# Attention, token and channel mixing, Fourier mixing: the mixing pass's second layer sums three features per addition instead of two

## The chip, the cores and the metric

The kernel runs on one core of a Trainium2 chip. The core has TensorE (PE, with its weight loads PEld), VectorE (DVE), ScalarE (ACT), GpSimd (POOL) and SyncE (SP, whose queue issues the DMA transfers). What counts is the device time of one execution in microseconds (us). PE writes its products into PSUM, an on-chip memory of banks of 128 x 512 fp32 numbers; DVE and ACT carry them on to SBUF.

## The reference, cut to what matters

```python
q_pool = q.reshape(B, H, S // 2, 2, D).mean(axis=3)          # B 4, H 8, S 1152, D 64
scores = scale * np.matmul(q_pool, k.transpose(0, 1, 3, 2))
attn = softmax(scores)
x = np.matmul(attn, v)                                       # -> x: 4 x 576 x 512
# token and channel mixing
h = np.maximum(x.transpose(0, 2, 1) @ w_tok1, 0.0) @ w_tok2  # 576 -> 256 -> 576
u = x + h.transpose(0, 2, 1)
x = u + np.maximum(u @ w_ch1, 0.0) @ w_ch2                   # 512 -> 1536 -> 512
# Fourier mixing, normalisation, a second channel layer
u = x + np.real(fft(fft(x, axis=1), axis=2))
un = (u - mean(u)) / np.sqrt(var(u) + 1e-6)
out = u + np.maximum(un @ w2_ch1, 0.0) @ w2_ch2              # 512 -> 2048 -> 512
```

## The kernel before, in words

All numbers are fp32. A product of full precision is made of three products of a faster format (fp32r): each operand is split into a high part, which ACT writes, and a low rest, which DVE or POOL writes; PE adds high x high, high x low and low x high in PSUM. So "three matmuls" below is one product.

The work has these parts:

- **Conversion** (`conv64`): the weights arrive as 64-bit floats and are turned into pairs of fp32r by ACT, POOL and DVE during the attention, and stored to DRAM.
- **Attention**, 32 heads in turn, 8 to a batch. From the ninth head on (`peaks`, `unit`) PE makes a tile of scores (L644, six matmuls into a region `m` of three banks), DVE finds each row's maximum (L651), ACT takes the exponent (L654) into a tile `s`; only then is `m` free for the next tile. PE turns `s` (L797, into a shared bank or the bank `tr`), ACT writes the high part `ph` (L801) and DVE the low part `pl` (L804), and PE multiplies both with the values into the one bank `av` (L811). ACT and DVE carry `av` to `xtr` (L821, L823), PE turns that (L843), DVE scales it (L855), and ACT and POOL write the batch's input of the mixing pass as `x` high and low (L858, L860).
- **Mixing pass** (`mix`), one for each of the 4 batches; the pass of a batch runs while the next batch's attention does, the last one with the Fourier part. Its PE work is a chain in one fixed order: the token layer (`r`, L916, then `u`, L944 and L951, with the sum `yt` begun from `u`), and then the channel layer with its 1536 features in 12 blocks of 128. First layer of block f: 12 + 12 matmuls (L981; tokens 0 to 255 and 256 to 575 apart, as everywhere here), then ACT (L902) and DVE (L905) write the block's high and low part to a buffer `h`. Second layer: for each of the two token ranges and four output blocks, PE sums two features' three matmuls each in one bank (six matmuls, L1001), and one DVE addition (L1010) adds the bank to `yt`. So six bursts of eight such groups make a pass. At its end `yt` is turned (L1035) and written out by ACT (L1040).
- **Fourier mixing, normalisation and the last channel layer** (L1157 to L1503) follow.

`banks` is a ring of three PSUM banks, from which `r`, `u`, the two channel layers, half of the turned scores and the turned heads all take. The buffers `h` are a ring of three, `ph` and `pl` rings of five, and the mixing weights come through a ring of five buffers `w` (L458, 512 KB each for the channel layer), which SP loads in the chain's order.

What stands where in each engine's queue is decided by a planner (`Plan.order`): it walks through all operations with assumed costs, and gives a free engine the ready operation with the smallest due time. The table `SHIFT` adds a number for each kind of operation to its due time; the numbers are so large that they act as priorities. On PE the second mixing layer (`yT`) goes ahead of scores (`M`) and of turning (`T`); the products with the values (`AV`) come behind these, and the first mixing layer (`hT`) last.

Of the kernel before, what the change touches and what calls it, by code (L numbers as in the profile page):

```python
# [11 lines left out]
F32R = mybir.dt.float32r  # L12
# [9 lines left out]
B, H, S, D = 4, 8, 1152, 64  # L22
# [9 lines left out]
PB = 5  # L32
# [7 lines left out]
NB = 3  # L40
NC = 2
NW = 5
NV = 3
NS = 6
ALONE = 8
NPH = 5
NPL = 5
UNITS = ((0, 256, (0, 1), ((0, 1), (2, 3), (4, 5), (6, 7), (8,))),
         (256, 320, (2, 3, 4), tuple((c,) for c in range(9))))
SPANS = ((0, 256), (256, 320))  # L50
# [9 lines left out]


SHIFT = {
    "cvld": -25.93, "cabs": 1270.21, "cclamp": 705.49, "cshift": 902.44, "csign": -44.94, "cexp": 832.42,
    "cword": 774.03, "cmul": -558.47, "cadd": 708.59, "chi": -53.24, "csub": -115.78, "cvst": -413.51, "cs":
    73.61, "warm.": -140.63, "l.": -1704.02, "q.": 351.07, "qh.": 1553.78, "ql.": 797.09, "kh.": -19.45, "kl.":
    1892.97, "M.": -2130.55, "mr.": 433.1, "zh.": -685.21, "mr2.": -1605.04, "zl.": -866.61, "mT.": 452.86,
    "mrow.": -843.49, "vld": -524.16, "S.": -408.9, "exp.": 741.3, "AV.": -1055.77, "xe.": -17.83, "turn":
# [7 lines left out]
    -425.22, "open": -1557.19, "sqrt": -2175.63, "fcld": -988.57, "fchi": 736.12, "fclo": -782.79, "nyld":  # L75
    -1351.45, "nyh": 186.74, "fld": 108.37, "FPUT": 625.26, "DFT": 33.71, "Zh": 1221.35, "Zl": 1190.62, "PB":
    -31.25, "PA": -31.11, "bs": -454.93, "pm": 280.63, "yadd": -483.73, "u2st": 617.43, "dwld": -491.2, "dwv":
    109.22, "dwh": -1442.53, "dwl": 2012.18, "mixover": -388.78, "fnetover": 785.38, "uld": -771.51, "bn":
    183.78, "bnr": 707.04, "un": 1261.22, "dturn": -317.55, "dth": -715.08, "dtl": -2596.93, "L": 157.31, "drl":
    185.99, "dll": 484.72, "dadd": 481.33, "dst": -84.03, "TB": 538.99, "TH": 2063.54, "TL": -508.2, "TA":  # L80
    641.51, "WR": 855.14, "WH": 262.43, "WL": -497.16, "VR": -355.27, "LP": 206.65, "LE": 459.2, "LC": -1185.38,
    "LH": 628.53, "LL": 257.54, "LQ": 1903.14,
}
PACE = 1.0307

# [147 lines left out]
def tile_attention_moe_fnet(  # L233
# [51 lines left out]
    with tc.manual_schedule():  # L285
# [52 lines left out]

        flow = [(0, 0), (0, 1), (0, 2)]
        for f in range(0, F1, 2):
            flow += [(1, f), (1, f + 1)] + [(0, x) for x in (f + 3, f + 4) if x < F1]
        cvw = Ring(NV, lambda: shelf.tile([128, 2048], F32, tag="slot", name="slot", bufs=NV))
        converted = []

# [516 lines left out]
            return turn, [a, o]  # L863


        h_r = ring(3, mp, [128, 2, NQ], F32R, "h")
        ut_r = ring(1, mp, [128, 2, 4, NQ], F32R, "ut")
        yt_r = ring(1, mp, [128, 4, NQ], F32, "yt")
        yo_r = ring(3, mp, [128, C], F32, "yo")
# [2 lines left out]
        def mix(b, xx, x_ops):  # L872
# [119 lines left out]
                    ]))  # L992

            def layer2(f):
                ww = {x: get((1, x)) for x in (f, f + 1)}
                for r, (t0, n) in enumerate(SPANS):
                    for cc in range(4):
                        mms = []
                        for x in ww:
                            for wi, hi in ((0, 0), (0, 1), (1, 0)):  # L1000
                                mms.append(lambda ps, k=len(mms), x=x, wi=wi, hi=hi, cc=cc, t0=t0, n=n: nc.tensor.matmul(  # L1001
                                    ps[:, :n], ww[x][2]("p (s n) -> p s n", s=2)[:, wi, 128 * cc:128 * cc + 128],
                                    hs[x][0].t[:, hi, t0:t0 + n], start=(k == 0), stop=(k == 5)))

                        def y(cc=cc, t0=t0, n=n):
                            return yt.t[:, cc, t0:t0 + n]

                        deps = [ww[x][0] for x in ww] + [o for x in ww for o in hs[x][1][r]]
                        y_ops[r] += group("y", mms, t_pe(1, n), deps, [ww[x][1] for x in ww] + [hs[x][0] for x in ww], [
                            ("V", t_dve(n), lambda ps, y=y, n=n: nc.vector.tensor_tensor(  # L1010
                                out=y(), in0=ps[:, :n], in1=y(), op=ALU.add), [], u_ops[r], [yt])])

            for layer, f in flow:
                if layer == 0:
                    layer1(f)
                elif f % 2 == 0:
                    layer2(f)

            y_stores, rest = [], list(chain)
# [679 lines left out]
```

## Time and profile before

| | |
|---|---|
| median of three runs (lowest, highest) | 1431.44 us (1429.68, 1437.26) |
| the profiled execution | 1428.16 us |
| its span, first to last instruction | 1426.2 us |
| PE busy in the span | 1379.3 us, 97% |
| DVE, ACT, POOL busy | 988.5, 763.6, 576.6 us |

The span is what the profile's rows divide up; the profiled execution's own time is 2.0 us more. An engine is busy while an instruction of it runs; PE's matmuls overlap, so that its mean duration of one is longer than the time from one to the next.

### The profile page before, as it was taken

What the parts mean: (1) busy time and instruction counts of PE and PEld (TensorE: products, weight loads), DVE (VectorE), ACT (ScalarE), POOL (GpSimd) and SP (SyncE); (2) the same over time, 40 slices, a digit from 0 to 9 for tenths busy, and PEclk for the clock granted to TensorE, in tenths of its full rate; (3) what the DMA queues carried; (4) which work ended last, traced back from release to release, by engine and by line L of the source; (5) the groups of instructions that cost most, each with busy time, mean ns of one, the idle gap of its engine ahead of it and who ended that gap; (6) DMA issues with size and microseconds to landing.
All of it is one profiled execution on the core that took longest, in us unless ns stands there. A gap on an engine that the chain in (4) does not pass through costs nothing.

```text
span 1426.2 us, 24338 instructions
## 1 busy us (share of the span) xinstructions
PE 1379.3 (97%) x9019; PEld 1270.3 (89%) x9019; DVE 988.5 (69%) x1830; ACT 763.6 (54%) x1534; POOL 576.6 (40%) x471
## 2 busy tenths in 40 slices
PE   7999999999999999999999999999999999999998
PEld 6777788999988999999989998999899898888887
DVE  7667578978877789786878885577647665455443
ACT  4555568767667866656866654322325443344332
POOL 4667767756755557666354665021210000000000
PEclk8999999999999999999999999999999999999999
DMA  6676776776578577667754457875266543644532
GB/s 183 195 217 195 208 202 201 226 233 206 155 222 259 150 215 245 201 204 229 202 182 141 148 177 251 255 230 157 67 213 210 194 140 141 215 165 142 201 113 91
DMA packets 112176, 270.34 MB, mean 190 GB/s; under 512 B 9971, under 2 KB 37748, under 8 KB 111767
## 3 DMA queue, kind: packets, MB, share of 16 engines
q1 hardware_dynamic: 112058, 268.79, 60.9%
q8 instruction: 71, 1.16, 0.3%
q14 instruction: 47, 0.39, 0.1%
HBM read 191.15 MB, written 44.86 MB: 165 GB/s over the span
## 4 chain that ended last, share of the span: by engine, by line
PE 86%; DVE 6%; ACT 3%; issue 2%; DMA 1%; POOL 1%; SPq 0%; ACTq 0%; DVEq 0%; POOLq 0%
PE bank L981 10%; PE bank L1001 10%; PE bank L1444 10%; PE m L644 9%; PE av L811 7%; PE y L1503 7%; PE c L1503 5%; PE av L758 4%; PE bank L797 4%; PE tr L797 3%; PE bank L678 3%; PE s L747 2%; PE bank L1314 2%; PE y L1336 2%; PE bank L916 2%; PE c L1157 2%
## 5 line engine op out<-in xcount | busy, mean ns | idle before, releaser
L651 DVE TENSOR_REDUCE nm<-m 128x1 f32<-128x1152 f32 (+1 forms) x120 | 162.4, 1353 | 49.2 <-PE m L644 47.6
L981 PE MATMUL bank<-ut,w 128*128 128x320 f32 (+1 forms) x1152 | 177.2, 298 | 5.0 <-DVE h L905 2.0
L981 PEld LDWEIGHTS bank<-ut,w 128*128 128x128 f32 x1152 | 160.2, 190 | 7.1 <-DVE h L905 2.6
L1001 PE MATMUL bank<-h,w 128*128 128x320 f32 (+1 forms) x1152 | 164.4, 297 | 1.0 <-DVE yt L1010 0.7
L1444 PE MATMUL bank<-tt,wc 128*128 128x320 f32 x1008 | 157.7, 311 | 4.3 <-DVE e L1458 3.8
L644 PE MATMUL m<-kk,qq 128*128 128x384 f32 (+1 forms) x720 | 156.7, 349 | 4.6 <-ACT s L654 4.4
L1444 PEld LDWEIGHTS bank<-tt,wc 128*128 128x128 f32 x1008 | 150.0, 188 | 11.9 <-DVE e L1458 8.9
L1001 PEld LDWEIGHTS bank<-h,w 128*128 128x128 f32 x1152 | 157.3, 189 | 2.7 <-DVE yt L1010 1.3
L654 ACT ACTIVATE s<-m,nm 128x1152 f32<-128x1152 f32 (+1 forms) x120 | 146.2, 1218 | 18.4 <-DVE nm L651 17.9
L368 POOL TENSOR_SCALAR slot<-slot 128x512 f32<-128x512 f32 (+2 forms) x62 | 119.7, 1935 | 55.6 <-ACT slot L366 46.6
L811 PE MATMUL av<-ph,vv 128*128 128x256 f32 (+1 forms) x432 | 131.2, 321 | 4.5 <-DVE xtr L823 4.4
L644 PEld LDWEIGHTS m<-kk,qq 128*128 128x128 f32 (+1 forms) x720 | 119.1, 182 | 10.6 <-ACT s L654 6.5
L801 ACT ACTIVATE ph<-bank 128x512 fp32r<-128x512 f32 (+1 forms) x192 | 89.6, 470 | 71.5 <-PE bank L797 69.8
L381 POOL TENSOR_TENSOR slot<-slot 128x512 f32<-128x512 f32 (+2 forms) x62 | 80.7, 1302 | 102.4 <-DVE slot L376 98.6
L811 PE MATMUL av<-pl,vv 128*128 128x256 f32 (+1 forms) x432 | 120.4, 296 | 1.3 <-DVE pl L804 1.3
L1458 DVE TENSOR_TENSOR e<-bank,e 128x320 f32<-128x320 f32 x96 | 47.1, 491 | 106.4 <-PE bank L1444 70.7
L1010 DVE TENSOR_TENSOR yt<-bank,yt 128x256 f32<-128x256 f32 (+1 forms) x192 | 86.0, 454 | 41.0 <-PE bank L1001 38.6
L1503 PE MATMUL y<-v,hp 128*128 128x512 f32 x432 | 103.9, 390 | 0.0
L804 DVE TENSOR_TENSOR pl<-bank,ph 128x512 fp32r<-128x512 f32 (+1 forms) x192 | 99.0, 522 | 3.1 <-ACT ph L801 2.7
L1454 ACT ACTIVATE e<-bank 128x320 f32<-128x320 f32 x72 | 31.3, 434 | 129.4 <-PE bank L1444 129.4
L801 ACT ACTIVATE ph<-tr 128x512 fp32r<-128x512 f32 (+1 forms) x144 | 70.4, 489 | 54.5 <-PE tr L797 44.9
L804 DVE TENSOR_TENSOR pl<-tr,ph 128x512 fp32r<-128x512 f32 (+1 forms) x144 | 79.2, 550 | 26.3 <-ACT ph L801 25.7
(162 smaller groups left out, 2956.9 us busy)
## 6 DMA issues: line engine op xcount, KB each, us to landing
w<-wb_d SPq DMA_DIRECT2D x96, 512.0 KB, 5.5
slot<-in_wm_dram SPq DMA_DIRECT2D x56, 512.0 KB, 6.0
v<-w_d SPq DMA_DIRECT2D x24, 1024.0 KB, 5.6
raw<-w_d SPq DMA_DIRECT2D x24, 896.0 KB, 5.7
kk<-kx SPq DMA_DIRECT2D x66, 288.0 KB, 5.1
wb_d<-slot SPq DMA_DIRECT2D x24, 512.0 KB, 2.6
v<-in_v_dram SPq DMA_DIRECT2D x32, 292.5 KB, 5.7
kx<-in_kT_dram SPq DMA_DIRECT2D x15, 576.0 KB
```

What stands on the lines that cost most here:

```text
L368: a = add("cclamp", "P", 0.155 + n * 0.00347, due, lambda: nc.gpsimd.tensor_scalar(out=f32(hi()), in0=f32(hi()), scalar1=F64_LO, scalar2=F ...
L644: nc.tensor.matmul(m.t[:n, :KW], qq.t[:r, t, q0:q0 + n], kk.t[:r, c * KW:(c + 1) * KW], start=(t == 0), stop=(t == 1))
L651: a = add("mx" + own_place, "V", t_dve(S), d + 0.05, lambda n=n, j=j: nc.vector.tensor_reduce(out=nm.t[:n, j:j + 1], in_=m_tile[0][:n, :, ...
L654: o = add("exp" + own_place, "A", t_act(S) + 0.18, d + 0.1, lambda s=s, n=n, j=j: nc.scalar.activation(out=s.t[:n].rearrange("p (c n) -> p ...
L797: nc.tensor.transpose(ps.t[:, at:at + r], made[j][0].t[:r, c * 128:(c + 1) * 128], ident[:r, :r])
L801: a = add("hi", "A", t_act(n), due + 0.1, lambda ps=ps, ph=ph, n=n: nc.scalar.activation(out=ph.t[:, :n], in_=ps.t[:, :n], func=AF.Copy), ...
L804: b = add("lo", "V", t_dve(n), due + 0.2, lambda ps=ps, ph=ph, pl=pl, n=n: nc.vector.tensor_tensor(out=pl.t[:, :n], in0=ps.t[:, :n], in1=f ...
L811: nc.tensor.matmul(po.t[:, :nq], vv.t[:, c].rearrange("p s d -> p (s d)"), x.t[:, k * nq:(k + 1) * nq], start=c == 0 and x is ph, stop=c = ...
L981: mms.append(lambda ps, k=len(mms), kk=kk, wi=wi, xi=xi, t0=t0, n=n: nc.tensor.matmul(ps[:, :n], view("p (s k n) -> p s k n", s=2, k=4)[:, ...
L1001: mms.append(lambda ps, k=len(mms), x=x, wi=wi, hi=hi, cc=cc, t0=t0, n=n: nc.tensor.matmul(ps[:, :n], ww[x][2]("p (s n) -> p s n", s=2)[:, ...
L1444: nc.tensor.matmul(ps.t[:, :PH], w.t[:, wi, k, 128 * kk:128 * kk + 128], x.t[:, xi, kk], start=(first and m == 0), stop=(last and m == 5), ...
L1503: nc.tensor.matmul(y.t, h.t[:, k, hi, j * 128:(j + 1) * 128], v.t[:, wi, k], start=(q == 0 and k == 0 and n == 0), stop=(q == 7 and k == 1 ...
```

## The change

The second layer now sums three features in a bank (nine matmuls) for each addition to `yt`. The order of the mixing chain follows: four first layers, then bursts of 72 second-layer matmuls with three first layers between them, where there were bursts of 48 with two between them. The ring `h` gets a fourth buffer; the rings `ph` and `pl` have four instead of five. All numbers of `SHIFT` are new, those of a kind mostly near the old ones; `PACE` and the rings `banks` and `w` stay.

```diff
+YF = 3
-NPH = 5
-NPL = 5
+NPH = 4
+NPL = 4
...
 SHIFT = {
-    "cvld": -25.93, "cabs": 1270.21, "cclamp": 705.49, "cshift": 902.44, "csign": -44.94, "cexp": 832.42,
+    "cvld": -90.22, "cabs": 1239.90, "cclamp": 939.59, "cshift": 946.77, "csign": -127.29, "cexp": 940.57,
...
-        flow = [(0, 0), (0, 1), (0, 2)]
-        for f in range(0, F1, 2):
-            flow += [(1, f), (1, f + 1)] + [(0, x) for x in (f + 3, f + 4) if x < F1]
+        flow = [(0, f) for f in range(YF + 1)]
+        for f in range(0, F1, YF):
+            flow += [(1, f + x) for x in range(YF)] + [(0, f + x) for x in range(YF + 1, 2 * YF + 1) if f + x < F1]
...
-        h_r = ring(3, mp, [128, 2, NQ], F32R, "h")
+        h_r = ring(YF + 1, mp, [128, 2, NQ], F32R, "h")
...
-                ww = {x: get((1, x)) for x in (f, f + 1)}
+                ww = {x: get((1, x)) for x in range(f, f + YF)}
...
-                                    hs[x][0].t[:, hi, t0:t0 + n], start=(k == 0), stop=(k == 5)))
+                                    hs[x][0].t[:, hi, t0:t0 + n], start=(k == 0), stop=(k == 3 * YF - 1)))
...
-                elif f % 2 == 0:
+                elif f % YF == 0:
```

What this moves is seen in the engines' queues. The names are those of the section on the kernel; in the changed kernel every line number is one higher (L1002 for L1001).

PE, in the first mixing pass, where a second-layer burst meets the attention. Before:

```order
L843 MATMUL bank<-ident,xtr_130 128x65 x5
L1001 MATMUL bank<-h,w 128x256 x6
L644 MATMUL m<-kk_147,qq_154 66x384 x4
L1001 MATMUL bank<-h,w 128x256 x12
L1001 MATMUL bank<-h,w 128x320 x12
L644 MATMUL m<-kk_147,qq_154 66x384 x2
L797 MATMUL tr<-ident,s 128x128 x4
L1001 MATMUL bank<-h,w 128x320 x12
```

The same place with the change:

```order
L982 MATMUL bank<-ut,w 128x320 x12
L645 MATMUL m<-kk_147,qq_154 128x384 x6
L1002 MATMUL bank<-h,w 128x256 x36
L1002 MATMUL bank<-h,w 128x320 x36
L645 MATMUL m<-kk_147,qq_154 128x384 x6
L798 MATMUL tr<-ident,s 128x128 x2
L798 MATMUL tr<-ident,s 128x66
L798 MATMUL bank<-ident,s 128x128 x2
```

Score matmuls (L644), a turned head (L843) and turned scores (L797) stood inside the burst of 48; the burst of 72 stands in one piece, with a whole tile's six score matmuls ahead of it and six behind it.

PE at the end of the attention, the last head's last products with the values and what follows. Before:

```order
L811 MATMUL av<-ph,vv 128x320
L811 MATMUL av<-pl,vv 128x320
L981 MATMUL bank<-ut,w 128x320 x9
L1001 MATMUL bank<-h,w 128x256 x3
L843 MATMUL bank<-ident,xtr_132 128x65 x5
L1001 MATMUL bank<-h,w 128x256 x21
L1001 MATMUL bank<-h,w 128x320 x24
L981 MATMUL bank<-ut,w 128x256 x12
L981 MATMUL bank<-ut,w 128x320 x12
L1001 MATMUL bank<-h,w 128x256 x24
L1001 MATMUL bank<-h,w 128x320 x24
L1035 MATMUL bank<-ident,yt 96x128 x4
```

With the change:

```order
L812 MATMUL av<-pl,vv 128x320
L812 MATMUL av<-ph,vv 128x320
L812 MATMUL av<-pl,vv 128x320
L812 MATMUL av<-ph,vv 128x320
L812 MATMUL av<-pl,vv 128x320
L1036 MATMUL bank<-ident,yt 96x128 x4
L1036 MATMUL bank<-ident,yt 97x128 x4
L1036 MATMUL bank<-ident,yt 96x128 x4
L812 MATMUL av<-ph,vv 128x320
L812 MATMUL av<-pl,vv 128x320
L844 MATMUL bank<-ident,xtr_132 128x65 x5
L917 MATMUL bank<-x_8802,w 128x512
```

Before, 117 matmuls of the third mixing pass (L981, L1001) stood between the last turned head (L843) and the turning of `yt` ahead of the fourth pass. Now the third pass is finished by then: only the turning of `yt` (L1036) is left between the last products with the values, and the fourth pass's first layer (L917) stands directly behind the turned head (L844), whose result it reads.

PE at the beginning of the third mixing pass, where the token layer ends (L944, L951) and two heads of the next batch, which wait for the pass to give its input `x` back, are turned. Before:

```order
L797 MATMUL tr<-ident,s 128x66
L644 MATMUL m<-kk_145,qq_148 128x384 x2
L843 MATMUL bank<-ident,xtr_130 128x65 x5
L644 MATMUL m<-kk_145,qq_148 128x384 x4
L843 MATMUL bank<-ident,xtr_132 128x65 x5
L811 MATMUL av<-ph,vv 128x320
L811 MATMUL av<-pl,vv 128x320
L811 MATMUL av<-ph,vv 128x320
L811 MATMUL av<-pl,vv 128x320
L797 MATMUL bank<-ident,s 128x128 x2
```

With the change:

```order
L952 MATMUL bank<-ident_r,x_5647 128x64
L945 MATMUL bank<-w,h 128x320
L798 MATMUL tr<-ident,s 128x128 x2
L798 MATMUL tr<-ident,s 128x66
L844 MATMUL bank<-ident,xtr_130 128x65 x5
L844 MATMUL bank<-ident,xtr_132 128x65 x5
L645 MATMUL m<-kk_145,qq_148 128x384 x6
L798 MATMUL bank<-ident,s 128x128 x2
L798 MATMUL bank<-ident,s 128x66
```

The two turned heads (L843) stood inside a tile of scores, with products with the values (L811) right behind; they now stand together, and a tile of scores and turned scores come ahead of those products.

## Rows read from the trace of the kernel before

**Rows 1.** the first part of the page: busy time, share and instructions of each engine.
```profile
PE 1379.3 (97%) x9019; PEld 1270.3 (89%) x9019; DVE 988.5 (69%) x1830; ACT 763.6 (54%) x1534; POOL 576.6 (40%) x471
```

**Rows 2.** windows, whole stages: busy us (x instructions), clock, DMA share.
```profile
0.00:177.00 177.00, 166.93 (x859) 129.82 (x860) 116.16 (x236) 92.81 (x175) 113.42 (x95) 0.97 0.71 200
177.00:858.00 681.00, 655.80 (x4799) 630.83 (x4798) 546.54 (x948) 463.98 (x954) 415.23 (x324) 0.99 0.67 200
858.00:1000.00 142.00, 139.93 (x1038) 136.15 (x1037) 93.21 (x226) 45.20 (x107) 35.04 (x38) 1.00 0.71 220
1000.00:1426.00 426.00, 416.65 (x2330) 373.54 (x2327) 232.54 (x421) 161.63 (x300) 12.94 (x15) 1.00 0.45 158
```

**Rows 3.** groups by line, whole span: line, operation, count | busy us, mean ns | idle before.
```profile
L1001 PE MATMUL bank<-h,w 128*128 128x320 f32 (+1 forms) x1152 | 164.4, 297 | 1.0 <-DVE yt L1010 0.7 <-DVE h L905 0.4
```

**Rows 4.** line L1010 alone: the additions to the running sum, and who waited for them.
```profile
L1010 DVE TENSOR_TENSOR yt<-bank,yt x192: 406/448/492, 270.9 to 1000.2; 128x256 f32<-128x256 f32 x96, 128x320 f32<-128x320 f32 x96
...
  PE bank L1001: 0.7, 2
```

**Rows 5.** who PE waited for: engine, line, then total us, times, longest us.
```profile
PE av L811 <- DVE xtr L823: 4.4, 3, 1.9
PE m L644 <- ACT s L654: 4.4, 6, 2.6
...
PE bank L797 <- DVE xs L855: 3.0, 2, 1.7
...
PE bank L981 <- DVE h L905: 2.0, 3, 0.8
PE bank L843 <- DVE pl L804: 2.0, 2, 1.3
```

**Rows 6.** windows about the two places where the granted clock fell.
```profile
186.00:192.00 6.00, 6.00 (x22) 5.63 (x23) 4.67 (x5) 4.86 (x9) 5.55 (x5) 0.52 0.23 92
...
712.00:718.00 6.00, 3.76 (x28) 2.98 (x27) 5.57 (x7) 5.78 (x12) 5.83 (x3) 0.96 0.56 179
718.00:724.00 6.00, 5.26 (x20) 5.27 (x21) 4.61 (x9) 0.80 (x2) 5.84 (x6) 0.50 0.17 69
```

**Rows 7.** timeline of PE at the end of the attention: start, us, instruction, idle before.
```profile
858.34 0.31 PE L811 MATMUL av<-pl,vv 128*128 128x320 f32 x1
...
860.16 0.47 PE L843 MATMUL bank<-ident,xtr 65*128 65x65 f32 x5
860.43 6.51 PE L1001 MATMUL bank<-h,w 128*128 128x256 f32 x45
...
869.99 5.82 PE L1001 MATMUL bank<-h,w 128*128 128x256 f32 x42
```

**Rows 8.** groups by line: PE, DVE, ACT and POOL steps of the attention.
```profile
L644 PE MATMUL m<-kk,qq 128*128 128x384 f32 (+1 forms) x720 | 156.7, 349 | 4.6 <-ACT s L654 4.4
...
L651 DVE TENSOR_REDUCE nm<-m 128x1 f32<-128x1152 f32 (+1 forms) x120 | 162.4, 1353 | 49.2 <-PE m L644 47.6 <-ACT ph L801 0.8
...
L823 DVE TENSOR_TENSOR xtr<-av,xtr 64x256 f32<-64x256 f32 (+1 forms) x48 | 22.1, 460 | 8.3 <-ACT xtr L821 7.0
...
L855 DVE TENSOR_TENSOR xs<-bank,rs 128x320 f32<-128x320 f32 x32 | 15.5, 483 | 1.8 <-PE bank L843 1.4
...
L654 ACT ACTIVATE s<-m,nm 128x1152 f32<-128x1152 f32 (+1 forms) x120 | 146.2, 1218 | 18.4 <-DVE nm L651 17.9
...
L801 ACT ACTIVATE ph<-tr 128x512 fp32r<-128x512 f32 (+1 forms) x144 | 70.4, 489 | 54.5 <-PE tr L797 44.9 <-DVE slot L373 2.4 <-PE av L811 2.0
...
L821 ACT ACTIVATE xtr<-av 64x256 f32<-64x256 f32 (+1 forms) x48 | 19.2, 400 | 17.9 <-PE av L811 17.4
...
L858 ACT ACTIVATE x<-xs 128x320 fp32r<-128x320 f32 x32 | 15.0, 468 | 8.9 <-DVE xs L855 8.9
...
L860 POOL TENSOR_TENSOR x<-xs,x 128x320 fp32r<-128x320 f32 x32 | 29.1, 913 | 10.3 <-ACT x L858 10.0
```

**Rows 9.** DMA issues: queue, count, KB each, median us from issue to landing.
```profile
w<-wb_d SPq DMA_DIRECT2D x96, 512.0 KB, 5.5
```

More of the change, by code (lines that the diff above doesn't have):

```diff
@@ L62 @@
 SHIFT = {
-    "cvld": -25.93, "cabs": 1270.21, "cclamp": 705.49, "cshift": 902.44, "csign": -44.94, "cexp": 832.42,
[L64 to L67, printed above, removed]
[7 rows of a table removed]
@@ L75 @@
[L75 to L79, printed above, removed]
@@ L80 @@
-    185.99, "dll": 484.72, "dadd": 481.33, "dst": -84.03, "TB": 538.99, "TH": 2063.54, "TL": -508.2, "TA":
-    641.51, "WR": 855.14, "WH": 262.43, "WL": -497.16, "VR": -355.27, "LP": 206.65, "LE": 459.2, "LC": -1185.38,
-    "LH": 628.53, "LL": 257.54, "LQ": 1903.14,
+    "cvld": -90.22, "cabs": 1239.90, "cclamp": 939.59, "cshift": 946.77, "csign": -127.29, "cexp": 940.57,
+    "cword": 897.99, "cmul": -625.82, "cadd": 599.51, "chi": 244.52, "csub": -253.97, "cvst": -337.88, "cs":
+    37.74, "warm.": -335.54, "l.": -1806.10, "q.": 351.4, "qh.": 1923.09, "ql.": 772.45, "kh.": -117.24, "kl.":
@@ new lines @@
+    2041.73, "M.": -2203.63, "mr.": 415.64, "zh.": -660.37, "mr2.": -1701.27, "zl.": -933.77, "mT.": 353.82,
+    "mrow.": -691.21, "vld": -731.14, "S.": -318.59, "exp.": 747.49, "AV.": -1354.90, "xe.": 160.69, "turn":
[7 rows of a table added]
+    "xa": -379.47, "open": -1345.52, "sqrt": -2195.89, "fcld": -948.73, "fchi": 627.8, "fclo": -529.7, "nyld":
+    -1118.59, "nyh": 276.62, "fld": -16.62, "FPUT": 697.76, "DFT": -18.42, "Zh": 1558.83, "Zl": 1137.18, "PB":
+    -31.17, "PA": -31.06, "bs": -579.47, "pm": 378.8, "yadd": -621.69, "u2st": 542.87, "dwld": -444.21, "dwv":
@@ L83 @@
+    178.26, "dwh": -1364.72, "dwl": 2146.06, "mixover": -160.23, "fnetover": 840.53, "uld": -782.98, "bn": -4.6,
+    "bnr": 906.88, "un": 980.22, "dturn": -187.73, "dth": -822.53, "dtl": -2446.47, "L": 278.88, "drl": 292.75,
+    "dll": 524.52, "dadd": 410.87, "dst": -170.79, "TB": 584.39, "TH": 2152.01, "TL": -355.49, "TA": 801.07,
+    "WR": 659.57, "WH": 448.57, "WL": -832.65, "VR": -645.8, "LP": 681.35, "LE": 335.61, "LC": -1200.07, "LH":
+    533.04, "LL": 297.33, "LQ": 1756.37,
 }
```

14 rows, old and new, of the table SHIFT are left out of this document.

## The prediction, made before the changed kernel ran

> **What bounds the kernel now.** I read the page's shares first, then the windows by stage, and then the waits of the engine that came out. PE is busy for 1379.3 of 1426.2 us [rows 1]; the 47 us in which it is not are all that a better order can win, and they are spread: 10.1 us before the mixing passes begin (0 to 177), 25.2 us while attention and mixing run together (177 to 858), 2.1 us in the fourth mixing pass, 9.4 us after it by window less busy time [rows 2]. DVE, which the change unloads, is busy for 546.5 of 681 us in the middle stage, so it is second there and not the bound. Who makes PE wait shows at which instructions DVE's load matters: the largest rows that DVE ends are the product bank carried away late (4.4 us), a turned head not yet scaled (3.0), the low part of a first-layer block (2.0) and the low part of the turned scores (2.0), together 11.4 us; another 4.4 us is a tile's exponent on ACT [rows 5]. The additions that the change thins out are hardly among them: PE waited 0.7 us for L1010 [rows 4], and sat idle 1.0 us ahead of all 1152 second-layer matmuls [rows 3].
>
> **The change part by part.**
>
> PE's own work: 1152 matmuls of L1001 before [rows 3], and after it 4 passes x 12 blocks x 8 groups x 3, the same. 0 us.
>
> The additions: 192 become 128, as 4 passes x 4 bursts x 8. One takes 0.448 us (median, [rows 4]), so DVE loses 64 x 0.448 = 28.7 us. Nothing on PE waits for that sum as such. What PE can win at this place is between nothing and the 1.0 us of [rows 3]; each addition now has nine matmuls of cover and not six (0.143 us each by 164.4/1152, so 1.3 and not 0.9 us, against 0.45). I take -0.5 us.
>
> DVE's other work comes earlier by that. Three of the four passes lie in the middle stage, so 48 additions or 21.5 us leave its 546.5, 4%. By proportion the 11.4 us of [rows 5] would shrink by 0.4; if all of these waits were the tail of a queue with additions in it, by 11.4. The waits are few and single (one to three times each), which puts the value near the lower end; but additions come in bursts of eight, so that a wait close to a burst loses more than its share: -2.0 us.
>
> The clock: at two places PE's granted clock falls to half (0.52 and 0.50, 1.2 GHz) for about 6 us, and at the second of them the profile shows PE busy for only 3.76 of the 6 us ahead [rows 6]. That is where the third pass's token layer holds the batch's input and attention stands still for it. At half rate 5.26 us of work is done that takes 2.6 at the full one. In the new order the two turned heads of that place stand together, and six score matmuls and three turned scores come between them and the products with the values, whose waits for their bank are the largest row of [rows 5]; so I count the spell as gone: -2.6 us, between that and 0. The first spell lies in the tiles' beginning at 177, where the order hardly changes; it stays.
>
> The end of the attention. Before, behind the last head's products (858.3) the turning (860.2) and all that follows it lie beside second- and first-layer work of the third pass, from 860.4 to about 877 [rows 7]. In the new order nothing of that pass is left there. PE must wait for ACT and DVE to carry the bank away before it can turn it, 0.40 + 0.46, and then for the scaling, the high and the low part before the fourth pass's first matmuls, 0.48 + 0.47 + 0.91 [rows 8]: 2.7 us in which nothing stands ahead on PE. The bounds are 0, if the turning of `yt` covers it after all, and 5.3, if this wait brings a spell at half rate like the one above. I take +2.7.
>
> Costed at nothing: the rings `ph` and `pl` with four buffers. ACT waited 2.0 us in all for PE to give a `ph` back for the bank `tr` [rows 8], and ACT is idle for a third of the stage [rows 2]; if that cover went, turned scores would come late and PE would wait at L811, as in the second window of [rows 6]. The weights: three second-layer ones now are needed at once, of five buffers. A load lands 5.5 us after its issue [rows 9]; the last of the three gets its buffer when the first of the three first-layer blocks is done, and then two blocks, 48 matmuls or 6.9 us at 0.143, stand ahead of its use. It is hidden with 1.4 us to spare. The fourth buffer `h` lets one block run ahead of a burst as before. In the first 177 us and in everything from the last channel layer on, PE's order is nearly or wholly the same: 0.
>
> The sum: -0.5 - 2.0 - 2.6 + 2.7 = -2.4 us. From the profiled execution's 1428.16 that is 1425.8. The median of the runs stands 3.3 us above the profiled one, so the time comes to **1429 us**. Half a per cent is 7.2 us, about what a measurement of this kernel can tell from no change; the forecast is: no change that can be told.
>
> **The rivals.**
>
> *Attention gets free of DVE's waits.* If the new order and the unloaded DVE take away the whole 11.4 us of [rows 5], the spell goes too, and the end of the attention stays covered by the turning of `yt`: 1428.2 - 0.5 - 11.4 - 2.6 = 1413.7, and 1417 as a median. For it speaks that PE is the bound everywhere, so that each wait removed counts in full; against it, that only 4% of DVE's work leaves the stage.
>
> *Attention runs out of cover* (slower). A burst of 72 now stands in one piece: at 6.51/45 us a matmul [rows 7] it is 10.4 us in which no tile of scores starts. Twelve such bursts are 125 of the 681 us that the attention's 120 tiles took, which leaves 4.6 us for each. A tile's own cycle is six matmuls, a maximum and an exponent, 156.7/120 + 1.35 + 1.22 = 3.9 us [rows 8], without waits in the queues of DVE and ACT. If those waits make it more than 4.6 us, this decides: the attention ends late, and there is no third-pass work left behind which it may. Before, some 16 us of it stood there. With a third of that as the delay (5 us, an estimate), the wait of 2.7 with a spell at half rate (5.3) and none of the gains but 0.5: 1438.0, and 1441 as a median. Against it speaks that the order was laid out with filling work between the bursts.
>
> *Weights come late.* SP issues in order; if the three loads in a row queue behind Fourier transfers, PE waits some 2 us at each of the fourth pass's three later bursts: +6 on the forecast, 1435, within half a per cent. For it speaks the DMA share of 0.71 in that window, against it the 1.4 us to spare.
>
> *More spells at half rate.* The second spell of [rows 6] follows a stretch with PE idle, and the new order has such stretches at the beginning of the later passes. The Trainium skill ("TensorE: Matmul & The Clock Gate", section "HAM oscillation — how this bites in real kernels") says that waits inside a loop can throw the array back to its cold clock each time round, and asks for work laid out without them; the trace agrees at the second of its two places, and no row shows more than the two. With the old spell kept and two new ones of 2.6 us the sum is +5.4, 1433.6 and 1437 as a median, still within half a per cent.
>
> **How the numbers follow.** The forecast has 0.43, attention freed 0.30, out of cover 0.19, late weights 0.04, more spells 0.04. So faster by over 0.5% (under 1424) has 0.30, slower by over 0.5% (over 1438.6) 0.19, and the three others within half a per cent make 0.51. The forecast's own range, from its bounds of 0 to -4 for DVE's relief and 0 to 5.3 at the attention's end, is 1424 to 1435. The range that leaves out one in ten on each side reaches to the first rival's 1417 with 2 us for its unknown end, and to just short of the second's 1441: **1415 to 1440**.
>
> **What would show it.** Right: L1010 with 128 executions and about 57 us; PE's idle time ahead of L1001 still near 1 us; in the window of the third pass's beginning a clock of 1.00; a wait of 2 to 3 us ahead of the fourth pass's L917, released by POOL or ACT. Wrong: PE idle in the middle stage well under 20 us (the first rival), or the score tiles ending much later than the 12 bursts explain and PE idle over 30 us (the second); waits of L1002 for a transfer (the third); more than two stretches at half clock (the fourth). The forecast itself fails if waits that I have taken from rows of before, because the new table moves every queue, lie at other places altogether.

## The result, and the profile after

The changed kernel takes 1442.68 us (median of 6 runs, 1439.0 to 1444.2), the kernel before 1431.84 beside it (6 runs, 1429.68 to 1437.26): a ratio of 1.0073, 95% interval 1.0051 to 1.0095. It is slower by 0.7%. The forecast was 1429 with a range to 1440, so it was wrong, in its sign and past its range. The profiled execution took 1442.44 us, its span is 1440.4. One of the four runs of e8 below took 3653.16 us, where the others took 1464.5 to 1466.2, and is left out of its figures.

The first part of the page after, then the windows of the stages (span's start to end; busy us of PE, PEld, DVE, ACT and POOL; granted clock; DMA share; GB/s). The attention now ends near 893 us, so the middle stage is cut there.

```profile
PE 1382.6 (96%) x9019; PEld 1271.8 (88%) x9019; DVE 956.5 (66%) x1766; ACT 763.5 (53%) x1534; POOL 575.1 (40%) x471
```
```profile
0.00:177.00 177.00, 165.36 (x851) 128.70 (x852) 113.32 (x238) 91.43 (x172) 109.61 (x93) 0.96 0.71 194
...
177.00:893.00 716.00, 682.03 (x4967) 653.74 (x4965) 536.74 (x928) 472.41 (x971) 435.81 (x341) 0.99 0.67 199
893.00:1000.00 107.00, 104.75 (x774) 101.97 (x774) 61.94 (x151) 35.04 (x85) 13.32 (x19) 1.00 0.78 237
...
1000.00:1440.00 440.00, 430.47 (x2432) 387.34 (x2430) 244.46 (x451) 164.62 (x308) 16.41 (x21) 1.00 0.44 155
```

The reader is to see three things. DVE did lose its work (988.5 to 956.5 us, 64 instructions), and PE has the same 9019 matmuls. PE's busy time grew by 3.3 us only: by the granted clock in windows of 2 us, PE ran at half rate (1.2 GHz) for 27.3 us after and 23.9 before, which is worth 1.7 us, and this difference lies in the first 36 us (clock 0.81 after, 0.86 before); from 177 us on it is 13.6 us in both. The other 1.6 us wasn't traced to a cause. The rest is PE standing still: span less busy time goes from 46.9 us [rows 1] to 57.8. By stage it was 10.1, 25.2, 2.1 and 9.4 us [rows 2]; it is now 11.6, 34.0, 2.2 and 9.5. So the middle stage, attention beside mixing, lost 8.8 of the 10.9 us.

The second layer's products and the additions after, by groups (line, shapes, count, busy us, mean ns, idle before):

```profile
L1002 PE MATMUL bank<-h,w 128*128 128x320 f32 (+1 forms) x1152 | 159.8, 298 | 2.8 <-issue 1.9 <-DVE yt L1011 0.5 <-DVE h L906 0.2
...
L1011 DVE TENSOR_TENSOR yt<-bank,yt 128x320 f32<-128x320 f32 x64 | 31.4, 490 | 36.3 <-PE bank L1002 35.9
L1011 DVE TENSOR_TENSOR yt<-bank,yt 128x256 f32<-128x256 f32 x64 | 27.0, 423 | 23.9 <-PE bank L1002 23.4
```

They did what the diff says: 128 additions, 58.4 us. Who PE waited for (us in total, times, longest):

```profile
PE m L645 <- ACT s L655: 10.1, 9, 2.9
...
PE tr L798 <- DVE pl L805: 3.5, 5, 1.4
PE bank L982 <- DVE h L906: 3.5, 4, 1.2
PE bank L798 <- DVE pl L805: 2.8, 5, 0.8
...
PE bank L945 <- DVE pl L805: 1.6, 3, 0.9
PE bank L917 <- ACT yo L1041: 1.6, 1, 1.6
...
PE av L812 <- DVE xtr L824: 0.4, 1, 0.4
```

Against [rows 5] the bank of the turned head (`xtr`, 4.4 us) got free as forecast, to 0.4. The tile of scores that waits for the exponential ahead of it went from 4.4 to 10.1, and waits for `pl` at the turning of scores, 1.2 us before, make 6.3 (all of PE's waits for `pl` together went from 7.1 to 10.7). Of the other rows that the prediction counted on, `xs` (3.0) and `pl` at the turned head (2.0) are gone, and `h` rose from 2.0 to 3.5: its four rows fell from 11.4 to 3.9 us, and other rows rose by more. Before and after, none of the large rows is an addition.

Where does it begin? From 177 to 300 us PE did 812 matmuls before and 754 after, with 4.1 us less of busy time in the row after (before first):

```profile
177.00:300.00 123.00, 116.19 (x812) 109.48 (x811) 98.86 (x162) 91.78 (x189) 84.27 (x59) 0.97 0.71 215
...
177.00:300.00 123.00, 112.13 (x754) 102.45 (x753) 90.77 (x152) 92.64 (x189) 90.35 (x62) 0.97 0.68 202
```

The first burst of the second layer starts at 297.8 us after (269.7 before). So the loss begins before a burst has run: 7.2 of the 10.1 us that tiles wait for the exponential lie in this window, where it was 3.3 before. It doesn't end there: PE's idle time grows by 4.1 us up to 300, shrinks by 2.5 from 300 to 440, and grows by 4.2 from 440 to 700 and by 3.0 from 700 to the attention's end (858 before, 893 after). But none of the nine waits for the exponential stands directly behind a burst; the three after 300 us (0.88 at 368, 1.69 at 729, 0.39 at 756) follow first-layer work, turned scores and products with the values.

### The profile page after: what moved, and what is told of

Same layout as the page of the kernel before. It is cut to its first block, busy times and chain, and to the rows that moved or that the text cites. A ratio compares the mean times of both kernels' runs of the same rounds, so it can differ in the third digit from the quotient of the medians.

```text
span 1440.4 us, 24289 instructions
## 1 busy us (share of the span) xinstructions
PE 1382.6 (96%) x9019; PEld 1271.8 (88%) x9019; DVE 956.5 (66%) x1766; ACT 763.5 (53%) x1534; POOL 575.1 (40%) x471
## 4 chain that ended last, share of the span: by engine, by line
PE 84%; DVE 5%; DMA 4%; ACT 3%; issue 2%; POOL 1%; SPq 1%; ACTq 0%; DVEq 0%; POOLq 0%
PE bank L1002 11%; PE bank L982 10%; PE bank L1445 10%; PE m L645 8%; PE y L1504 7%; PE av L812 6%; PE c L1504 5%; PE bank L798 3%; PE av L759 3%; PE tr L798 3%; PE bank L679 2%; PE bank L1315 2%; PE y L1337 2%; PE s L748 2%; PE bank L917 2%
## 5 line engine op out<-in xcount | busy, mean ns | idle before, releaser
L652 DVE TENSOR_REDUCE nm<-m 128x1 f32<-128x1152 f32 (+1 forms) x120 | 162.6, 1355 | 47.5 <-PE m L645 42.3
L645 PE MATMUL m<-kk,qq 128*128 128x384 f32 (+1 forms) x720 | 155.6, 349 | 10.2 <-ACT s L655 10.1
L1002 PE MATMUL bank<-h,w 128*128 128x320 f32 (+1 forms) x1152 | 159.8, 298 | 2.8 <-issue 1.9
L1002 PEld LDWEIGHTS bank<-h,w 128*128 128x128 f32 x1152 | 156.5, 191 | 4.0 <-issue 2.2
L802 ACT ACTIVATE ph<-bank 128x512 fp32r<-128x512 f32 (+1 forms) x192 | 89.3, 470 | 45.6 <-PE bank L798 32.3
L805 DVE TENSOR_TENSOR pl<-bank,ph 128x512 fp32r<-128x512 f32 (+1 forms) x192 | 99.5, 524 | 14.4 <-ACT ph L802 13.2
L1011 DVE TENSOR_TENSOR yt<-bank,yt 128x256 f32<-128x256 f32 (+1 forms) x128 | 58.4, 457 | 60.2 <-PE bank L1002 59.3
L802 ACT ACTIVATE ph<-tr 128x512 fp32r<-128x512 f32 (+1 forms) x144 | 70.6, 490 | 50.9 <-PE tr L798 47.4
L1504 PEld LDWEIGHTS y<-v,hp 128*128 128x128 f32 x432 | 80.5, 188 | 16.4
```

Source lines behind the costliest of these rows:

```text
L645: nc.tensor.matmul(m.t[:n, :KW], qq.t[:r, t, q0:q0 + n], kk.t[:r, c * KW:(c + 1) * KW], start=(t == 0), stop=(t == 1))
L652: a = add("mx" + own_place, "V", t_dve(S), d + 0.05, lambda n=n, j=j: nc.vector.tensor_reduce(out=nm.t[:n, j:j + 1], in_=m_tile[0][:n, :, ...
L802: a = add("hi", "A", t_act(n), due + 0.1, lambda ps=ps, ph=ph, n=n: nc.scalar.activation(out=ph.t[:, :n], in_=ps.t[:, :n], func=AF.Copy), ...
L805: b = add("lo", "V", t_dve(n), due + 0.2, lambda ps=ps, ph=ph, pl=pl, n=n: nc.vector.tensor_tensor(out=pl.t[:, :n], in0=ps.t[:, :n], in1=f ...
L1504: nc.tensor.matmul(y.t, h.t[:, k, hi, j * 128:(j + 1) * 128], v.t[:, wi, k], start=(q == 0 and k == 0 and n == 0), stop=(q == 7 and k == 1 ...
```

## The experiments

The order in which each engine's instructions stand is written by the planner from costs, ring sizes and the table `SHIFT`. "Order" below is the theory that the time was lost by writing a new order where the old one had been fitted; "rings", "bursts", "form" and the others are its rivals. This table gathers the profiled executions; PE has 9019 matmuls in each, so the third column shows mostly clock (in e7 the mean granted clock is 0.976, before 0.992) and the fourth PE's idle time. The ratio is to the kernel before on the same chip, with its 95% interval.

| run | span | PE busy | rest | ratio |
|---|---|---|---|---|
| before | 1426.2 | 1379.3 | 46.9 | 1 |
| changed | 1440.4 | 1382.6 | 57.8 | 1.0073 (1.0051 to 1.0095) |
| e1 new form, old table | 1446.5 | 1388.6 | 57.9 | 1.0168 (1.0149 to 1.0186) |
| e2 old form, new table | 1443.6 | 1385.6 | 58.0 | 1.0132 (1.0112 to 1.0153) |
| e3 before, rings of four | 1446.7 | 1389.7 | 57.0 | 1.0161 (1.0143 to 1.0179) |
| e4 before, thin additions | 1425.1 | 1379.2 | 45.9 | 1.0002 (0.9983 to 1.0022) |
| e5 order of e3, five tiles | 1446.7 | 1390.0 | 56.7 | 1.0143 (1.0105 to 1.0181) |
| e6 before, table moved by 5 | 1444.4 | 1386.8 | 57.6 | 1.0100 (1.0078 to 1.0122) |
| e7 before, table moved by 20 | 1459.6 | 1401.5 | 58.1 | 1.0182 (1.0149 to 1.0215) |
| e8 changed, scores first | 1462.7 | 1399.8 | 62.9 | 1.0244 (1.0218 to 1.0270) |
| e9 changed, thin maxima | 1438.6 | 1385.9 | 52.7 | 1.0052 (1.0025 to 1.0079) |
| e10 before, thin maxima | 1415.8 | 1375.9 | 39.9 | 0.9915 (0.9891 to 0.9939) |
| e11 changed, thin additions | 1442.6 | 1383.4 | 59.2 | 1.0069 (1.0040 to 1.0098) |
| e12 changed, table moved by 5 | 1453.3 | 1390.3 | 63.0 | 1.0183 (1.0157 to 1.0208) |
| e13 changed, keys behind | 1441.5 | 1385.3 | 56.2 | 1.0094 (1.0074 to 1.0114) |
| e14 changed, loads behind | 1443.8 | 1387.1 | 56.7 | 1.0100 (1.0069 to 1.0131) |
| e15 changed, thin maxima and keys behind | 1433.5 | 1384.3 | 49.2 | 1.0031 (1.0015 to 1.0047) |
| e16 before, loads behind | 1426.2 | 1378.6 | 47.6 | 1.0006 (0.9985 to 1.0027) |
| e17 before, other move of 5 | 1444.8 | 1383.5 | 61.3 | 1.0112 (1.0078 to 1.0146) |
| e18 changed, same move as e17 | 1450.6 | 1386.1 | 64.5 | 1.0176 (1.0132 to 1.0220) |

### Form, table and rings apart

e1 is the changed kernel with the table of before, e2 the kernel before with the table of the change. e3 is the kernel before with

```diff
-NPH = 5
-NPL = 5
+NPH = 4
+NPL = 4
```

> The changed kernel with the numbers of SHIFT of the kernel before; three features per addition, four buffers h and the rings of four stay. Before is 1431.8 us, the change 1442.7. If the loss comes from the new numbers (table), this is near 1432, and PE's waits for the exponent at L644 fall from 10.1 to about 4 us. If it comes from the form (long bursts, or the smaller rings), this is near 1442 with those waits still near 10.

> The kernel before with the numbers of SHIFT of the changed kernel; two features per addition, three buffers h and rings of five. If the loss comes from the new numbers, near 1442; if from the long bursts or the smaller rings, near 1432.

> The kernel before with rings ph and pl of four instead of five buffers, nothing else; its order is planned anew. If the smaller rings take away the work that PE puts between two tiles of scores, 1437 or more and waits at L644 well over 4.4 us; if the rings are free, as the prediction costed them, within 3 us of 1431.8.

Medians: 1452.02, 1445.51 and 1450.38 us. No part alone is harmless: the table without the form costs 1.3%, four tiles a ring without anything else 1.6%. The table of the change fits its form better than the old one does (1442.7 against 1452.0), and the old one fits the old form better. What the three have in common is that the planner had to write a new order. e1 and e2, each with the other's table, stand 6.5 us apart, the new form above.

e5 takes the very order of e3 and gives each ring its fifth tile back:

```diff
-... early_p["p"].tile([128, 512], F32R, tag=t, name=t, bufs=n) ...
+... early_p["p"].tile([128, 512], F32R, tag=t, name=t, bufs=5) ...
```

> The kernel before, planned as if the rings ph and pl had four tiles (the very order of the run e3_rings_of_four, 1450.4 us), but each ring has five real tiles, so that a tile is free one use earlier than the order needs. Theory 'order': the cost lies in the order that the planner wrote, not in a wait for a tile of the ring: 1450, within 4 us. Theory 'rings': the engines wait for a tile of ph or pl in the run: most of the 21 us comes back, 1428 to 1438, and PE's waits at the turning of scores for pl fall from 5.0 us towards the 0.3 us of before.

1451.11 us. ACT's wait until PE gives a tile `ph` back shows that the fifth tile was there (us in total, times, longest; the kernel before, the changed one, e3, e5):

```profile
ACT ph L801 <- PE av L811: 3.2, 9, 0.7
...
ACT ph L802 <- PE av L812: 13.8, 23, 1.4
...
ACT ph L801 <- PE av L811: 16.5, 18, 3.8
...
ACT ph L801 <- PE av L811: 0.8, 3, 0.4
```

The tiles are free in e5 and nothing comes back, and PE's wait for `pl` at the turning is 5.0 us as in e3. In the kernel before, a ring of four costs by the order that is written for it, not by a wait for a tile. A fifth tile in the changed kernel's own order wasn't tried, nor the reverse, before's order with four tiles.

### How much a new order costs by itself

e6, e7 and e17 leave the kernel before as it is and move the numbers of its table at random (`PB`, `PA` and `DFT` stay), as here the first ones of e17:

```diff
-    "cvld": -25.93, "cabs": 1270.21, "cclamp": 705.49, ...
+    "cvld": -25.73, "cabs": 1272.53, "cclamp": 703.19, ...
```

> The kernel before with all its work, rings and tiles, but each number of the planner's table (except the two of the second mixing layers and the one of the mixing by frequencies that stand almost unmoved in the change) moved by a random amount of standard deviation 5; the change moved them by 147. Theory 'order' (before's order is one fitted point, and any other order loses what the fitting had won): 1435 to 1455, as with the new table or the rings of four. Theory 'rings and form' (the order is worth little; the structural edits cost the time): 1425 to 1434.

> The same with a standard deviation of 20 and other random numbers. Theory 'order': as much as in e6_table_moved_by_5 or more, 1438 to 1460, with the loss at other places of the span than there. Theory 'rings and form': 1425 to 1436.

> The kernel before with its table moved at random by a standard deviation of 5, other random numbers than in e6_table_moved_by_5 (1444.9). Theory 'order': 1438 to 1458 again, so that e6 was no accident.

1444.87, 1456.35 and 1445.96 us. The work, the tiles and the form are those of before, and 14 to 26 us are lost. In the table above, PE's idle time rises by 10.7 to 14.4 us in these three, the whole size of the change's loss. So far theory "order" holds: before's order is a fitted point with 46.9 us of idle time, and the other orders of its form that were tried have 56.7 to 61.3.

e12 and e18 do the same to the changed kernel, with the random numbers of e6 and of e17.

> The changed kernel with every number of its table but the same three moved at random with standard deviation 5. Theory 'order' (the change's table too is a fitted point of its own): slower than the changed kernel, 1447 to 1465. If the change's table had not been fitted to its form, a move of 5 would do as often good as harm: 1437 to 1447.

> The changed kernel with its table moved by the same random numbers as e17_before_other_move_of_5. Theory 'form' (the changed form is slower in any order of like fit): 8 to 16 us above e17. Theory 'order alone': between 6 below and 6 above e17.

1456.45 and 1453.65 us, 14 and 11 above the changed kernel. So its table is fitted too, and theory "order" can't be the whole of the loss: the changed kernel isn't short of a fit. The pairs with like moves stand 11.6 and 7.7 us apart, the fitted pair 10.8: the second misses the 8 that theory "form" asked for by a little, and "order alone" (within 6) by more. With e1 and e2 that makes four pairs, all with the changed form above, by 6.5 to 11.6 us; every run of e18 (1452.3 to 1459.3) is above every one of e17 (1445.0 to 1448.7). The changed form seems to be some 6 to 12 us slower at a like fit. Orders of one form differ by 1 to 3 us at the same size of move (e6 and e17, e12 and e18) and by 11 between sizes (e6 and e7), and the ratio intervals of e17 and e18 still meet: the pairs lean that way and don't settle the size.

### DVE's relief

e4 and e11 thin the additions of both kernels in their own orders:

```diff
-out=y(), in0=ps[:, :n], in1=y(), op=ALU.add)
+out=y()[:, :8], in0=ps[:, :8], in1=y()[:, :8], op=ALU.add)
```

> The kernel before, in its own order, but each addition L1010 works on 8 columns instead of 256 or 320, so that the rest of the running sum lacks the second layer. The 192 additions should take some 0.15 us instead of 0.45: about 57 us off DVE, twice what the change takes off. By the prediction's price (2.5 us for 28.7) it is 1427; if all the waits that DVE ends go, 1420; if relief of DVE is worth nothing to PE, 1431 to 1432.

> The changed kernel in its own order, its 128 additions to the running sum (L1011, 457 ns) on 8 columns only, so 29 us or so of DVE's work is left out. Theory 'DVE is late as a whole': what helps DVE helps PE, 1434 to 1439. Theory 'the waits are those of single chains, with the additions not among them', as in e4_thin_additions: 1442, within 3.

1428.56 us (ratio 1.0002) and 1442.23. Both leave most of the second layer out of the sum. In e4, DVE does 47.5 us less, more than the change takes from it, and the time stands still; the prediction's four rows of waits are 4.5, 3.0, 2.0 and 2.0 us, 11.5 against 11.4. What the additions give back goes for the most part into DVE's idle time ahead of the next of them (41.0 us before, 80.7 in e4).

The same was then tried on DVE work that stands in a chain PE waits for, the maximum of a tile of scores (e10 in the kernel before, e9 in the changed one):

```diff
-in_=m_tile[0][:n, :, :KW], axis=AX.XY, op=ALU.max, negate=True)
+in_=m_tile[0][:n, :, :8], axis=AX.XY, op=ALU.max, negate=True)
```

> The changed kernel in its own order, but each maximum of a tile of scores (L652, 120 times 1355 ns) looks at 8 of every 384 columns, so it is left out in the main: DVE loses some 130 us, and the way from a tile's last product to its exponential is about a microsecond shorter. Theory 'waits' (the new order lays a tile of scores too close behind the one ahead and turned scores too close behind DVE's queue; that is PE's 10.9 us of added idle time): the 10.1 us for m and most of the 10 us for pl go, 1426 to 1434, and the distance to the kernel before with the same edit shrinks from 11 to 5 us or less. Theory 'elsewhere' (the loss is in the structure, such as banks held by longer sums): 1436 to 1442, distance still 9 or more.

> The kernel before in its own order with the same edit (L651 looks at 8 of every 384 columns). Its waits for m are 4.4 us and those for DVE's queue few. Theory 'waits': it gains less than the changed kernel does, 2 to 6 us, 1423 to 1428. Theory 'elsewhere': the same gain in both, whatever its size.

1437.11 and 1417.33 us. Here DVE's relief (126 us in e10, 120 in e9) does count: 14 us before, but less than half of that after (5.6 by the medians, 0.2% by the ratios, whose intervals overlap), the reverse of what theory "waits" expected, and the distance grows from 11 to 20. Theory "waits" in that form falls. The waits of e9 say why. With the maximum out of the way the wait for the exponential grew, from 10.1 to

```profile
PE m L645 <- ACT s L655: 16.4, 15, 3.0
```

while the waits for `pl` fell from 6.3 to 1.5. So something other than the maximum holds the exponential. (e10 beats both kernels, but a maximum over 24 of 1152 columns doesn't bound the exponents, so it is no kernel to keep.)

### Bursts

e8 changes one number in the changed kernel, so that tiles of scores go ahead of the second layer's bursts:

```diff
-"yT": -449.71
+"yT": 0.0
```

> The changed kernel with one number of its table changed: the second layer's products come due 450 later than the change has them, so tiles of scores go ahead of its bursts and the bursts are cut into shorter pieces between them. Theory 'bursts' (long bursts of the second layer hold tiles of scores back, the slower rival of the prediction): 1430 to 1437, and PE's wait for the maxima of scores (m, 10.1 us) falls to about 5. Theory 'order': the change of one number is one more new order, no nearer to before's: 1438 to 1460, and no wait has a reason to fall.

1465.75 us, the slowest order of all and above what either theory expected, and the wait for `m` is 10.9 us and not 5. The time alone doesn't settle theory "bursts", since e8 is one more rewritten order; but the bursts are cut (one into pieces of 36, 27 and 9 matmuls with tiles of scores between them, from 388 to 401 us) and the wait that they were to cause is still there. At one place a burst rather covers a wait: at 427 us ACT waits 6.3 us for a load and PE, in a burst of L1002, loses nothing.

### A late load in ACT's queue

What held the exponential is seen on ACT in the changed kernel. The timeline's columns are start, duration, instruction and the idle time before it with its releaser; ACT first, then PE at the same place:

```profile
212.05 0.39 ACT L962 ACTIVATE ut<-bank 128x256 fp32r<-128x256 f32 x1 [1.01 <-PE bank L945]
214.08 1.16 ACT L601 ACTIVATE kx<-kx 128x1152 fp32r<-128x1152 f32 x1 [1.65 <-DMA kx<-in_kT_dram]
215.15 1.20 ACT L655 ACTIVATE s<-m,nm 128x1152 f32<-128x1152 f32 x1
```
```profile
213.35 0.44 PE L798 MATMUL bank<-ident,s 128*128 128x128 f32 x3
216.49 1.67 PE L645 MATMUL m<-kk,qq 128*128 128x384 f32 x6 [2.70 <-ACT s L655]
```

The tile's maximum was done at 211.7. ACT's next instruction is the copy of the next pair's keys, whose load has not landed; ACT stands 1.65 us, copies for 1.1 us, and only then comes the exponential that PE needs. It costs PE 2.70 us, and a spell at half rate follows: the four microseconds after have a granted clock of 0.57, 1.2 GHz for most of them, where the 17 before had 1.00:

```profile
200.00:217.00 17.00, 13.77 (x94) 12.69 (x93) 10.31 (x19) 10.57 (x22) 13.19 (x9) 1.00 0.84 236
217.00:221.00 4.00, 4.00 (x21) 3.71 (x19) 2.98 (x5) 2.58 (x7) 4.00 (x4) 0.57 0.67 246
```

The same stands at 727 us (ACT idle 2.06, PE 1.69). In all ACT waited 10.7 us for loads of keys after, and 1.3 before. The Trainium skill ("TensorE: Matmul & The Clock Gate", section "HAM oscillation — how this bites in real kernels") describes a loop in which each wait of the array is followed by work at its half clock; the row at 217 agrees in kind, with a single wait.

e13 lets the exponential pass the copy of the keys on ACT, at four places, and leaves all other engines' order alone. e14 does it for the first step of conversions too, e16 the same to the kernel before, and e15 is e13 with thin maxima.

```diff
-        for o in self.order():
+        for o in behind(self.order()):
...
+def behind(out):
+    for o in [o for o in out if o.key in ('kh',) and o.eng == "A"]:
+        i = out.index(o)
+        ahead = [k for k in range(i + 1, len(out)) if out[k].eng == "A"][:2]
+        hit = [k for k in ahead if out[k].key in ('exp',)]
+        if hit and not any(o in x.deps + x.after for x in out[i + 1:hit[-1] + 1]):
+            out.insert(hit[-1], out.pop(i))
+    return out
```

> The changed kernel, PE, DVE, POOL and SP in its own order; on ACT, at four places, the copy of the next pair's keys (L601, 1.16 us, which waits for its load) trades places with the exponential (L655) that stands one or two behind it. Theory 'late load in ACT's queue': the waits of 2.70 us at 216.5 and 1.69 us at 729.5 go, and the half-rate spell of 3.4 us right after the first (1.7 us) with them: 1434 to 1438; PE's wait for m falls from 10.1 to about 5.5 us. Rival 'made good elsewhere': the exponential comes early but PE meets the next wait of its chain a few tiles on: 1440 to 1444 with the wait for m lower all the same.

> As e13_after_keys_behind, and at some eight more places the first ACT step of a weight conversion (L380, which waits for its load too) goes behind the exponential that stands one or two behind it. Theory 'late load in ACT's queue': a further 0.4 to 3 us, 1432 to 1437. Rival: the conversions come later and the weights with them, no gain over e13_after_keys_behind or a loss of some us.

> The changed kernel with thin maxima (as e9_after_thin_maxima, 1437.1) and the keys' copy behind the exponential at the same four places. Theory 'late load in ACT's queue': the late load was what ate the gain of the thin maxima; the waits of 2.78 us at 215.9, 1.61 at 544.6 and 2.98 at 721.5 go if they are among the four places: 1427 to 1432, and the wait for m falls from 16.4 to under 10. Rival: 1435 to 1439.

> The kernel before with the same exchange on ACT alone (copies of keys and first steps of conversions behind an exponential that stands one or two behind them, some dozen places). Its ACT waited 1.3 us in all for loads of keys, so theory 'late load in ACT's queue' has little to win there: 1425 to 1432, the same within 0.3%. Rival 'any exchange disturbs a fitted order': 1435 or more.

1443.02, 1444.99, 1433.30 and 1431.32 us. In e13 the two waits are gone and the sum of that row falls from 10.1 to 6.5 us, but not the time. At the first place ACT and PE now read:

```profile
211.04 1.22 ACT L655 ACTIVATE s<-m,nm 128x1152 f32<-128x1152 f32 x1
...
212.56 1.17 ACT L601 ACTIVATE kx<-kx 128x1152 fp32r<-128x1152 f32 x1 [0.21 <-issue]
...
214.21 0.42 ACT L802 ACTIVATE ph<-bank 128x320 fp32r<-128x320 f32 x1
```
```profile
212.40 1.34 PE L645 MATMUL m<-kk,qq 128*128 128x384 f32 x6
215.20 1.07 PE L945 MATMUL bank<-w,h 128*128 128x256 f32 x5 [1.46 <-DVE pl L805]
```

The tile starts at once, but the copies still stand ahead of the turned scores (L802), so `pl` is late and PE waits 1.46 us two groups on. The spell at half rate stays too (215 to 219 us, clock 0.58), which the expectation had counted as gone with the wait of 2.70 us. The waits of e13 show it in sum:

```profile
PE m L645 <- ACT s L655: 6.5, 7, 2.9
PE tr L798 <- DVE pl L805: 4.6, 6, 1.3
PE bank L982 <- DVE h L906: 4.5, 4, 2.2
...
PE bank L945 <- DVE pl L805: 3.1, 4, 1.5
```

3.6 us went from the first row, and 3.6 came back in the others; PE's busy time is 2.7 us longer. The rival "made good elsewhere" holds for e13 alone. With thin maxima, which give those next waits room, the same exchange is worth 3.8 us (1437.11 to 1433.30, though the two intervals overlap, so this size is not sure): e15 missed the expected 1427 to 1432 by 1.3, and its wait for `m` fell to 8.6. The late load is real, and it seems to be one of several limits that lie close behind one another. e14 won nothing more, and e16 shows that an exchange of a dozen places on one queue doesn't by itself disturb the kernel before: the losses of e6 and e17 seem to need more of the order rewritten.

## Why the prediction was wrong

- **PE's work, 0:** right, 1152 products and 9019 matmuls as before.
- **The additions, -0.5:** the count and the time were right (128, 58.4 us, forecast 57), the gain was nothing (e4).
- **"DVE's other work comes earlier", -2.0:** wrong. The proportion that it started from looked at DVE's load; e4 took 47.5 us away and won 0.0%, and the four rows stayed. Waits on DVE are waits for single chains, and the additions are in hardly any of them (e10: 126 us in a chain are worth 14). In the changed kernel the four rows did shrink, from 11.4 to 3.9 us, by the new order and not by DVE's relief.
- **The half-rate spell, -2.6:** right at its place and wrong in sum. Where the third pass begins (660 to 740 us) the clock after is 1.00, and the `xtr` wait is gone. But the rival "more spells" came true: from 177 us on the kernel before has two spells of 6.8 us at half rate, the changed one four of 3.4 us (from 190, 217, 316 and 617), 13.6 us in both. Each of the four follows about 1 us behind one of PE's four longest waits there (2.87, 2.70, 1.77 and 1.92 us). So the term is 0.
- **The end of the attention, +2.7:** right in size, and in part by luck. PE stands 1.00 us ahead of the turned head and 1.57 ahead of the fourth pass, 2.6 in sum; the rows name ACT's `yo` as what ended both:

```profile
892.51 0.52 PE L844 MATMUL bank<-ident,xtr 65*128 65x65 f32 x5 [1.00 <-ACT yo L1041]
894.61 7.34 PE L917 MATMUL bank<-x,w 128*128 128x512 f32 x30 [1.57 <-ACT yo L1041]
```
```profile
891.55 0.43 ACT L822 ACTIVATE xtr<-av 64x320 f32<-64x320 f32 x1 [1.71 <-PE av L812]
891.88 0.58 ACT L1041 ACTIVATE yo<-bank 96x512 f32<-96x512 f32 x1
893.60 0.47 ACT L859 ACTIVATE x<-xs 128x320 fp32r<-128x320 f32 x1 [1.14 <-DVE xs L856]
893.97 1.06 ACT L1041 ACTIVATE yo<-bank 97x512 f32<-97x512 f32 x2
```
```profile
892.01 0.49 DVE L824 TENSOR_TENSOR xtr<-av,xtr 64x320 f32<-64x320 f32 x1 [2.02 <-ACT xtr L822]
893.07 0.49 DVE L856 TENSOR_TENSOR xs<-bank,rs 128x320 f32<-128x320 f32 x1 [0.57 <-PE bank L844]
```

The first wait is the forecast one: the bank `av` is carried away until 892.50 (L822, L824), 0.04 us later than `yo`, and L844 starts at 892.51. In the second, the scaling and the high part took their turn as forecast, until 894.07, but then PE waited for a bank that `yo` emptied, and not for the low part on POOL (0.87 us, priced at 0.91), which ended at 895.01, behind the first matmul of L917.

- **The weights, 0:** right; no row of waits has L1002 behind a load. Its one long wait, 1.92 us at 615.5 for which the row names no releaser, ends 0.1 us after DVE's `pl` (L805) at 615.41, which stood behind a conversion step of 2.86 us (L377) and a maximum.
- **"Costed at nothing", and with it all waits that a new order makes: this is the step that failed.** The prediction changed PE's waits only at the places where it had looked at the orders, took their prices from rows of before, and put the rest of some 5000 matmuls in the middle stage at 0. Measured, PE's idle time rose by 10.9 us, 8.8 of them in that stage, mostly in waits that were small before: tiles for the exponential from 4.4 to 10.1 us, `pl` at the turning of scores from 1.2 to 6.3. For the rings `ph` and `pl` it asked whether ACT or PE would wait for a tile. ACT does (13.8 us after, 3.2 before), but in e3, where that wait is 16.5 us, taking it away won nothing (e5); and still the rings alone cost 1.6% (e3), since the planner writes another order for them. A rewritten order of the kernel before stands 14 to 26 us above the fitted one (e2, e3, e6, e7, e17), and a table of its own wins part of that back (e1 to the changed kernel, 9 us). The prediction's last sentence named this as what would fail it, and gave it no chance and no price.
- **The rival "attention runs out of cover"** gave 1441, near the time, by another way: the attention does end late (893 and not 860), but no wait for the exponential follows a burst, and the loss begins ahead of the first one. Scores first made it no better (e8).

What stays open is why the changed kernel, with a table that fits it, is still 10.8 us above the kernel before. The pairs lean to the form itself (6.5 to 11.6 us), but which part of it, the longer groups, the chain's order or the rings of four, no run shows. That a load is late on ACT's queue was shown at two places; for the other waits of the middle stage no single cause was shown.

## What to carry to other kernels

Where an order is written by a planner and fitted by a table, an edit of ring sizes or groupings is also a new order, and its price is measured by moving the table a little with nothing else changed; here that was 14 us and more, where the edit was forecast to win 2.4. A relief on an engine that isn't the bound is priced by the chain in which the work stands, not by its busy share: thin it and look. When one wait is taken away, look which wait stands next behind it before its length is counted as a gain.

## What was not expected of the hardware

Removing 47.5 us of VectorE's work changed the time by 0.02% (interval -0.17% to +0.22%), and removing 126 us changed it by 0.85% in one order, and 120 us by less than half of that in another. Clock and idle time come apart in the table: over all rewritten orders of the kernel before, idle time is 56.7 to 61.3 us, while PE's busy time for the same matmuls runs from 1383.5 to 1401.5. In e7 the busy time so rose by more (22 us, at a mean granted clock of 0.976 against 0.992) than the idle time (11).
